# Three edits to a chunked recurrence kernel: which engine copies the transposed block inverses, which engine fills a block-diagonal tile, and when one product is placed on VectorE

## The chip, the cores and the metric

The kernel runs on one core of a Trainium2 chip. A core has TensorE (PE in the profile, with its weight loads as PEld), VectorE (DVE), ScalarE (ACT), GpSimd (POOL) and SyncE (SP), which here issues the DMAs. Each engine works through its own queue in order. The metric is device time in microseconds (us); lower is better. "q" behind an engine's name means its sequencer.

## The reference

Three layers follow one another. Nearly everything the change touches lies in the first, a recurrence over 768 tokens for 4 x 8 heads with a 40 x 40 state each:

```python
for t in range(S):
    y[:, :, t] = np.einsum('bhd,bhde->bhe', rt, state)
    Sa = np.einsum('bhde,bhe->bhd', state, at)
    state_decay = state * wt[:, :, None, :] - np.einsum('bhd,bhe->bhde', Sa, bt)
    state = state_decay + np.einsum('bhd,bhe->bhde', vt, kt)
...
h = np.maximum(x @ w_in, 0.0)              # second layer: 3-tap convolution over tokens, sigmoid gate
return (h * gate @ w_out).astype(np.float32)
...
gated = u * v_s                            # third layer: token mixing of a normalised half, then w_out
return (gated @ w_out).astype(np.float32)
```

All data are float32.

## The kernel before

The recurrence is computed in chunks. Tokens fall into 6 groups of 128 (two chunks of 64), and a group with one of the 4 batch entries is a unit, so there are 24 units of 8 heads. The main loop runs over the units; in pass `kk` it interleaves generators for different units in 19 parts, in the order of the string `CDCBDDCBDACAABBAADD`:

- A (unit `kk+9`): transposes `a` and P to make `bdA` and PT, and multiplies them (L174, masked into G at L175). PT comes from P by transposes on PE (L167), and P must by then be multiplied by the inverse decays `il` (function `l_pm`, L145, on VectorE).
- B (unit `kk+1`): builds `bdN`, a 128 x 128 tile per head that holds four 32 x 32 inverse blocks on its diagonal and two products beside them, and multiplies with it (L295, tile `pw`). The four diagonal quarters are copied from DT (L278); the block beside them is copied from `px` by ACT (L287). Before, quarters 1 and 3 are GpSimd's and quarters 0 and 2 VectorE's. There is one `bdN`.
- C (unit `kk`): the recurrence itself. For each of two chunks PE forms `pu` (L327), ACT copies it to ZU (L329), GpSimd copies that to UR (L331), PE forms the tile `pm` (L338, not the function `l_pm`), and VectorE adds and scales it (L339, L341). The next `pu` needs L341's output.
- D (units `kk-1` and `kk`): the output of the unit. Its masks are SS (L373).

Beside these, a generator `subst(n)` inverts the 32 x 32 triangular blocks of group n on VectorE, two operations per row (L206 multiplies, L208 adds), handed out at 1.25 operations per part. At its end a transposed copy LT of the inverses L is made (L211), stored to memory, and read back by `loadD` as DT. The group 0 copy of LT is VectorE's, those of groups 1 to 5 are ACT's. In group 0 (`SMALL`) a shorter form is used, and L278 is not executed.

The list SCHED says behind which part of a pass a prefetch step is put. `[5,"pm"]` puts `l_pm` behind part 5 of every odd pass up to pass 13 (of pass 1 four parts later), that is P for the pair of units whose A starts four parts on. VectorE, ACT and SP run in the order written here. From pass 14 on the weights of the second layer are split into high and low parts in the gaps (L551 to L604). The output of the recurrence goes through memory to the second and third layers, which run on PE at nearly full load.

Of the kernel before, what the change touches and what calls it, by code (L numbers as in the profile page):

```python
# [11 lines left out]
def attention(tc, keep, ident, vr,bk,w,a, x, spare=None):  # L12
    nc=tc.nc
    B,H,S,D=w.shape
    C=64; HB=32; NU=S//128; HC=C//2; H2=2*H; NP=B//2
    sy=nc.sync; V=nc.vector; T=nc.tensor; G_=nc.gpsimd; AC=nc.scalar
    with ExitStack() as ctx:
# [24 lines left out]
        for q in range(4):  # L42
            qs=slice(q*HB,(q+1)*HB)
# [43 lines left out]
        def later(m,f):  # L87
            due.append((now[0]+m,f)); 
        def tick():
            now[0]+=1  # L90
            for d in [d for d in due if d[0]<=now[0]]:
                due.remove(d); d[1]()
# [92 lines left out]
        def subst(n):  # L185
            if n not in Ls: Ls[n]=(sb.tile([128,HB*HB+HB],F32,name="L"),sb.tile([128,HB*HB//4],F32,name="tmp"),sb.tile([128,HB,HB],F32,name="LT"))
            flat,tmp,LT=Ls[n]
            L=flat[:,0:HB*HB].rearrange("p (t j) -> p t j",j=HB)
            BQ[0].dma_start(out=L,in_=tb_d[n])
            yield  # L190
            if n in SMALL:
                K=HB//2
                V.memset(L[:,K:,0:K],0.0)
                Q=flat.rearrange("p (s r) -> p s r",s=2)[:,:,0:K*HB].rearrange("p s (t j) -> p s t j",j=HB)[:,:,:,0:K]
                for j in range(1,K-1):
                    m=K-1-j
                    t=tmp[:,0:2*m*j].rearrange("p (s m k) -> p s m k",s=2,m=m)
                    V.tensor_tensor(t,Q[:,:,j+1:,j:j+1].to_broadcast([128,2,m,j]),Q[:,:,j:j+1,0:j].to_broadcast([128,2,m,j]),ALU.mult)
                    yield
                    V.tensor_tensor(Q[:,:,j+1:,0:j],Q[:,:,j+1:,0:j],t,ALU.add)  # L200
                    yield
            else:
                for j in range(1,HB-1):
                    m=HB-1-j
                    t=tmp[:,0:m*j].rearrange("p (m k) -> p m k",m=m)
                    V.tensor_tensor(t,L[:,j+1:HB,j:j+1].to_broadcast([128,m,j]),L[:,j:j+1,0:j].to_broadcast([128,m,j]),ALU.mult)  # L206
                    yield
                    V.tensor_tensor(L[:,j+1:HB,0:j],L[:,j+1:HB,0:j],t,ALU.add)  # L208
                    yield
            V.memset(flat[:,0:HB*HB:HB+1],1.0)  # L210
            (V.tensor_copy if n==0 else AC.copy)(LT,L.rearrange("p t j -> p j t"))  # L211
            def put():
                BQ[0].dma_start(out=dt_d[n],in_=LT)
                BQ[0].dma_start(out=dd_d[n],in_=L if n in SMALL else L[0:128:2])
                stored.update((n,j) for j in range(2))
            later(DDL,put)
            yield
        inv={}; stored=set()
        def loadD(p):

            if p>=NK//2: return
            n,j=p//2,p%2
            if (n,j) not in stored: return later(1,lambda: loadD(p))
            DT=sb.tile([128,H2,HB],F32,name="DT",bufs=1); D1=sb.tile([128,H2,HB],F32,name="D1",bufs=1)
            hs=slice(j*H2*4,(j+1)*H2*4)
            BQ[0].dma_start(out=DT,in_=dt_d[n][hs].rearrange("(b h q) t j -> (q t) (b h) j",b=2,q=4))
            if n in SMALL: BQ[0].dma_start(out=D1,in_=dd_d[n][hs].rearrange("(b h q) t j -> (q t) (b h) j",b=2,q=4))
            for c in range(0 if n in SMALL else 2):
                BQ[0].dma_start(out=D1[c*C:c*C+HB],in_=dd_d[n][j*H2*2:(j+1)*H2*2].rearrange("(b h q) t j -> q t (b h) j",b=2,q=2)[c])
            inv[n,j]=(DT,D1)  # L230
        def Bp(kk):

            i,n=units[kk]
            u=st[kk]; G=pair[n,i//2]['G']; h0=(i%2)*H
            DT,D1=inv[n,i//2]
            N=bdN[0]
            F=sb.tile([96,H,HB],F32,name="F",bufs=1)
            quarters=[slice(q*HB,(q+1)*HB) for q in range(4)]
            if n in SMALL:
                K=HB//2  # L240
                pe=ps.tile([128,H,K],F32,tag="ps",name="pe")
                for h in range(H):
                    for q,qs in enumerate(quarters):
                        T.matmul(pe[q*HB:q*HB+K,h],lhsT=G[qs,h0+h,q%2*HB:q%2*HB+K],rhs=DT[qs,h0+h,K:],start=True,stop=True)
                for q in range(4):
                    AC.copy(FI[q*HB:q*HB+K,:,K:],pe[q*HB:q*HB+K])
                yield
                pg=ps.tile([128,H,HB],F32,tag="ps",name="pg"); pd=ps.tile([96,H,HB],F32,tag="ps",name="pd")
                for h in range(H):
                    for qs in quarters: T.matmul(pg[qs,h],lhsT=D1[qs,h0+h],rhs=FI[qs,h],start=True,stop=True)  # L250
                for q in (1,3):
                    qs=quarters[q]
                    AC.copy(N[qs,:,q*HB:(q+1)*HB],pg[qs])
                for h in range(H):
                    for qs in quarters[::2]: T.matmul(pd[qs,h],lhsT=FI[qs,h],rhs=D1[qs,h0+h],start=True,stop=True)
                X0=sb.tile([96,H,HB],F32,name="X0",bufs=1)
                for q in (0,2):
                    qs=quarters[q]
                    V.tensor_copy(N[qs,:,q*HB:(q+1)*HB],pg[qs])
                    AC.copy(X0[qs],pd[qs])  # L260
                if i%2==1: later(DTLS,lambda: loadD(kk//2+1))
                yield
                right=lambda h,c: N[c*C+HB:c*C+C,h,c*C+HB:c*C+C]
                left=lambda h,lo: X0[lo,h]
            else:
                right=lambda h,c: DT[c*C+HB:c*C+C,h0+h]
                left=lambda h,lo: D1[lo,h0+h]
            pf=ps.tile([128,H,HB],F32,tag="ps",name="pf")
            for h in range(H):
                for c in range(2):  # L270
                    lo=slice(c*C,c*C+HB); hi=slice(c*C+HB,c*C+C)
                    T.matmul(pf[lo,h],lhsT=G[hi,h0+h,0:HB],rhs=right(h,c),start=True,stop=True)
            for c in range(2):
                lo=slice(c*C,c*C+HB)
                AC.copy(F[lo],pf[lo])
            for q in range(0 if n in SMALL else 4):
                qs=quarters[q]
                (G_.tensor_copy if q%2 else V.tensor_copy)(N[qs,:,q*HB:(q+1)*HB],DT[qs,h0:h0+H])  # L278
            yield
            px=ps.tile([128,H,HB],F32,tag="ps",name="px")  # L280
            for h in range(H):
                for c in range(2):
                    lo=slice(c*C,c*C+HB)
                    T.matmul(px[lo,h],lhsT=left(h,lo),rhs=F[lo,h],start=True,stop=True)
            for c in range(2):
                lo=slice(c*C,c*C+HB)
                AC.copy(N[lo,:,c*C+HB:c*C+C],px[lo])  # L287
            if i%2==1 and n not in SMALL: later(DTL,lambda: loadD(kk//2+1))
            yield
            WT=u['WT']=[]  # L290
            for g in range(2):
                W=sb.tile([104,4,128],F32,name="WT",bufs=4); WT.append(W)
                p=ps.tile([128,4,128],F32,tag="ps",name="pw")
                for j in range(4):
                    T.matmul(p[:104,j],lhsT=G[:,h0+g*4+j,C:],rhs=N[:,g*4+j],start=True,stop=True)  # L295
                AC.mul(W,p[:104],-1.0)
                yield
# [94 lines left out]
        def pump(m):  # L392
            while m>0 and (bg or bg2):
                q=bg or bg2
                try: next(q[0])
                except StopIteration: q.pop(0); continue
                m-=1
# [10 lines left out]
        with tc.manual_schedule(engines={mybir.EngineType.SP,mybir.EngineType.DVE,mybir.EngineType.Activation}):  # L408
# [30 lines left out]
            l4=lam_prep(4); next(l4)  # L439
            mixed(2,l2,W[3]); l_dup(2); l_g(2); mixed(3,l2,W[4]); flush()  # L440
            s0=subst(0); next(s0)
            lms['lam',2](); lms['lam',3]()
            next(l4)
# [12 lines left out]
            flush()  # L456
            l_il(4)
            sub1=subst(1); next(sub1)
            l_P(4)
            b0=Bp(0)  # L460
            for _ in range(4): next(b0); steps(l4,W[9])
            loadV(0)
# [7 lines left out]
            with tc.manual_schedule():  # L470
# [9 lines left out]
                for kk in range(NK):  # L480
                    i,n=units[kk]
# [6 lines left out]
                    for g in ORDER if kk<TAIL else ORDER2:  # L488
# [8 lines left out]
                        tick(); acc+=RATE0 if kk<3 else RATE if kk<14 else RATE2; pump(int(acc)); acc-=int(acc)  # L497
                        for s,f in SCHED[(kk+LA+1)%2]+SCHEDC[kk%2]:
                            if s==z:
# [20 lines left out]
RATE=1.25  # L520
RATE2=1.25
RATE0=1.4
SCHED=[[[1, "il"], [11, "araw"], [12, "ln"], [14, "g"], [15, "dup"], [16, "P"], [17, "ar"]], [[5, "pm"]]]
SCHEDC=[[[6, "Z"]], [[10, "V"]]]
SUB=5
TBL=3
# [543 lines left out]
```

## Time and profile before

| | |
|---|---|
| three runs | 956.01 us median (954.18 to 960.27) |
| the profiled execution | 954.4 us, of which the span is 952.7 us |
| PE busy over the span | 90% |
| VectorE, ACT, GpSimd busy | 70%, 56%, 21% |
| the recurrence's main loop | from about 95 to 476 us of the span |
| second and third layers | from about 476 us to the end |

A row of a timeline gives the start and the time taken in us, the engine, the line, the operation, the tiles written and read, the shape, and how many instructions are merged; in brackets stands how long the engine was idle just before and which instruction ended that idle time.

### The profile page before, as it was taken

To read this page: it belongs to the slowest core of one execution; us is meant where nothing else is said; L and a number is where in the kernel's file an instruction comes from. 1 tells how busy PE (TensorE), PEld (TensorE's weight loads), DVE (VectorE), ACT (ScalarE), POOL (GpSimd) and SP (SyncE) were. 2 spreads that over 40 slices of the span, in tenths; PEclk is the share of its full clock that TensorE was granted. 3 is DMA by queue.
4 is the path that set the end of the run, shared out by engine and by line. 5 is a ranking of instruction groups with operands and counts; after the bars stand their busy time and mean duration, and the time that the engine had idled before them with its cause. 6 is when DMAs were issued, how large, how long until landed. Compare 5 with 4: busy or idle time off the path is not lost. (4 is left out here: it accounts for less than half of the span.)

```text
span 952.7 us, 23475 instructions
## 1 busy us (share of the span) xinstructions
PE 855.6 (90%) x9575; PEld 791.0 (83%) x9575; DVE 662.5 (70%) x1503; ACT 536.8 (56%) x1166; POOL 204.7 (21%) x268
## 2 busy tenths in 40 slices
PE   0888689999989999899777799999999899998997
PEld 0577588988989888799766699998999889998997
DVE  6877784794876959876659976378725877368841
ACT  0463577768777765778555653366515654266521
POOL 2110011121211111233300102144123441234221
PEclk9975799999999998899889999999999999999999
DMA  8989794646557444244131320111001100011001
GB/s 216 211 208 208 158 207 110 152 97 155 112 115 161 90 121 112 79 130 113 60 108 66 98 81 26 36 49 35 27 22 42 57 0 26 21 53 32 1 1 46
DMA packets 149189, 86.70 MB, mean 91 GB/s; under 512 B 124176, under 2 KB 138256, under 8 KB 147152
## 3 DMA queue, kind: packets, MB, share of 16 engines
q1 hardware_dynamic: 148800, 84.78, 36.1%
q8 instruction: 77, 1.26, 0.6%
q14 instruction: 40, 0.33, 0.1%
q10 hardware_dynamic: 272, 0.33, 0.1%
HBM read 61.24 MB, written 23.86 MB: 89 GB/s over the span
## 5 line engine op out<-in xcount | busy, mean ns | idle before, releaser
L693 PE MATMUL psp<-spt,vv 128*128 128x384 f32 x576 | 105.6, 338 | 0.5 <-DVE vv L821 0.3
L693 PE MATMUL ph<-XT,G 128*128 128x386 f32 x512 | 102.6, 346 | 0.7 <-DVE XT L726 0.7
L693 PEld LDWEIGHTS psp<-spt,vv 128*128 128x128 f32 x576 | 100.2, 188 | 2.2 <-ACT vv L818 1.0
L693 PEld LDWEIGHTS ph<-XT,G 128*128 128x128 f32 x512 | 93.8, 194 | 1.1 <-DVE XT L726 1.0
L769 PE MATMUL acc<-gh,G 128*128 128x384 f32 x320 | 71.3, 349 | 16.0 <-ACT gh L753 9.3
L755 POOL TENSOR_TENSOR gl<-c,gh 128x384 fp32r<-128x384 f32 x48 | 66.2, 1379 | 89.8 <-ACT gh L753 78.2
L769 PEld LDWEIGHTS acc<-gh,G 128*128 128x128 f32 x320 | 56.5, 192 | 24.5 <-ACT gh L753 13.4
L331 POOL COPY ZU<-ZU 64x320 f32<-64x320 f32 x48 | 24.9, 519 | 222.8 <-ACT ZU L329 216.7
L838 DVE TENSOR_TENSOR psp<-psp,bb 128x384 f32<-128x384 f32 x32 | 18.1, 566 | 70.6 <-PE psp L693 70.5
L753 ACT CAST gh<-c 128x384 fp32r<-128x384 f32 x64 | 33.0, 515 | 52.2 <-DVE c L751 50.8
L751 DVE TENSOR_TENSOR c<-h,c 128x384 f32<-128x384 f32 x64 | 39.3, 613 | 33.2 <-ACT c L748 33.0
L208 DVE TENSOR_TENSOR L<-L,tmp 128x30 f32<-128x30 f32 (+9 forms) x150 | 57.6, 384 | 4.0
L174 PE MATMUL p<-PT,bdA 80*128 80x128 f32 x384 | 55.1, 304 | 3.4 <-ACT PT L168 3.3
L372 PE MATMUL pS<-bdR,ZV 80*128 80x128 f32 x384 | 55.3, 288 | 2.4 <-ACT ZV L366 2.4
L206 DVE TENSOR_TENSOR tmp<-L 128x30 f32<-128x30 f32 (+9 forms) x150 | 52.5, 350 | 7.0 <-DMA L<-tb 3.0
L174 PEld LDWEIGHTS p<-PT,bdA 80*128 80x128 f32 x384 | 51.7, 216 | 6.4 <-ACT PT L168 6.3
L295 PE MATMUL pw<-bdN,G 128*104 128x128 f32 x384 | 54.6, 303 | 1.2 <-issue 1.1
L842 ACT CAST zh<-u 128x384 fp32r<-128x384 f32 x28 | 14.4, 515 | 73.1 <-DVE u L839 73.1
L295 PEld LDWEIGHTS pw<-bdN,G 128*104 128x104 f32 x384 | 51.2, 196 | 2.1 <-issue 1.3
L175 DVE TENSOR_TENSOR G<-p,mT 128x512 f32<-128x512 f32 x48 | 32.8, 688 | 28.1 <-PE p L174 27.7
L372 PEld LDWEIGHTS pS<-bdR,ZV 80*128 80x128 f32 x384 | 47.7, 195 | 3.9 <-ACT ZV L366 2.8
L843 POOL TENSOR_TENSOR zl<-u,zh 128x384 fp32r<-128x384 f32 x28 | 28.6, 1022 | 101.0 <-ACT zh L842 89.8
(185 smaller groups left out, 2104.1 us busy)
## 6 DMA issues: line engine op xcount, KB each, us to landing
P<-in_bk_dram SPq DMA_DIRECT2D x12, 640.0 KB, 5.5
ZU<-in_vr_dram SPq DMA_DIRECT2D x12, 640.0 KB, 7.2
lq<-in_w_dram SPq DMA_DIRECT2D x12, 320.0 KB, 6.5
araw<-in_a_dram SPq DMA_DIRECT2D x12, 320.0 KB, 6.8
lam<-lq SPq DMA_DIRECT2D x12, 320.0 KB, 4.4
lnA<-lam SPq DMA_DIRECT2D x12, 320.0 KB, 7.4
ilam<-lq SPq DMA_DIRECT2D x12, 320.0 KB, 5.6
il<-ilam SPq DMA_DIRECT2D x24, 160.0 KB, 4.3
```

The lines of the kernel that those rows point to most:

```text
L174: T.matmul(p3[:,j],lhsT=bdA[:,g*4+j].rearrange("p c t -> p (c t)"),rhs=PTs[g][:,j],start=True,stop=True)
L175: V.tensor_tensor(G[:,hs,0:2*C],p3,mT.rearrange("p a t -> p (a t)").unsqueeze(1).to_broadcast([128,4,2*C]),ALU.mult)
L206: V.tensor_tensor(t,L[:,j+1:HB,j:j+1].to_broadcast([128,m,j]),L[:,j:j+1,0:j].to_broadcast([128,m,j]),ALU.mult)
L208: V.tensor_tensor(L[:,j+1:HB,0:j],L[:,j+1:HB,0:j],t,ALU.add)
L295: T.matmul(p[:104,j],lhsT=G[:,h0+g*4+j,C:],rhs=N[:,g*4+j],start=True,stop=True)
L372: T.matmul(p[:,j].rearrange("p c t -> p (c t)"),lhsT=ZV[:,j,0:2*C],rhs=bdR[:,j].rearrange("p c t -> p (c t)"),start=True,stop=True)
L693: L.tc.nc.tensor.matmul(out,lhsT=l,rhs=r,start=start and i==0,stop=stop and i==len(prs)-1)
L751: V.tensor_tensor(c,h[:,1:TH+1],c,ALU.mult)
L753: AC.copy(gh,c)
L755: def low(v): v.tensor_tensor(gl,c,gh.bitcast(F32),ALU.subtract)
L769: nc.tensor.matmul(acc[m],lhsT=l,rhs=r,start=f==0 and z<5 and z in (0,1,3),stop=f==NF-1 and z>=5)
L843: nc.gpsimd.tensor_tensor(gl,u,gh.bitcast(F32),ALU.subtract)
```

## The change

Three edits. LT is copied by VectorE in every group, where ACT made it for groups 1 to 5. All four quarters of `bdN` are copied by GpSimd, where two of them were VectorE's. And `l_pm` stands behind part 3 of the odd passes, where it stood behind part 5.

```diff
@@ subst
             V.memset(flat[:,0:HB*HB:HB+1],1.0)
-            (V.tensor_copy if n==0 else AC.copy)(LT,L.rearrange("p t j -> p j t"))
+            V.tensor_copy(LT,L.rearrange("p t j -> p j t"))
@@ Bp
             for q in range(0 if n in SMALL else 4):
                 qs=quarters[q]
-                (G_.tensor_copy if q%2 else V.tensor_copy)(N[qs,:,q*HB:(q+1)*HB],DT[qs,h0:h0+H])
+                G_.tensor_copy(N[qs,:,q*HB:(q+1)*HB],DT[qs,h0:h0+H])
@@ constants
-SCHED=[[...], [[5, "pm"]]]
+SCHED=[[...], [[3, "pm"]]]
```

On ACT one row goes at the end of each inversion; here in group 2, where the D part's ZV and the C part's ZU stand around it.

```order
@@ -151,5 +150,4 @@
 L362 ACTIVATE bdR<-pz,mB 80x4x64 x2
 L366 COPY ZV<-pv 80x4x104
-L211 COPY LT<-L 128x1024
 L329 COPY ZU<-pu 64x4x40 x2
 L287 COPY bdN<-px 32x8x32 x2
```

The ZU copy now stands right behind the ZV copy. VectorE takes LT behind the last step of the inversion and ahead of the second SS:

```order
@@ -264,4 +260,5 @@
 L373 TENSOR_TENSOR SS<-pS,mS 128x512
 L210 MEMSET L 128x32
+L211 COPY LT<-L 128x1024
 L373 TENSOR_TENSOR SS<-pS,mS 128x512
 L339 TENSOR_TENSOR pm<-pm,VM 40x320
```

The two instructions behind it, SS and the addition to `pm`, now stand behind LT. On VectorE in pass 5 (and 9 and 13) two `bdN` copies go and P's product moves up:

```order
@@ -224,10 +222,9 @@
 L206 TENSOR_TENSOR tmp<-L 128x238
 L208 TENSOR_TENSOR L<-L,tmp 128x14x17
-L278 COPY bdN<-DT 32x8x32 x2
 L206 TENSOR_TENSOR tmp<-L 128x234
+L145 TENSOR_TENSOR P<-P,il 128x1280
 L208 TENSOR_TENSOR L<-L,tmp 128x13x18
 L373 TENSOR_TENSOR SS<-pS,mS 128x512
 L206 TENSOR_TENSOR tmp<-L 128x228
-L145 TENSOR_TENSOR P<-P,il 128x1280
 L208 TENSOR_TENSOR L<-L,tmp 128x12x19
```

P's product stands ahead of SS and three steps of the inversion that it followed. PE's order is the same in both kernels, and so is SP's. On GpSimd each of the 20 bursts of copies doubles, always in the place of the first two; here one in the weight stretch (L604 is the low part of a weight):

```order
 L605 MEMSET G 64x512
 L331 COPY ZU<-ZU 64x8x40
-L278 COPY bdN<-DT 32x8x32 x2
+L278 COPY bdN<-DT 32x8x32 x4
 L331 COPY ZU<-ZU 64x8x40
 L604 TENSOR_TENSOR G<-mo,G 128x320 x2
```

Two more copies now stand ahead of the UR copy (L331) of the unit's second chunk.

## Rows read from the trace of the kernel before

**Rows 1.** The page: span, busy time of each engine over it.

```profile
span 952.7 us, 23475 instructions
PE 855.6 (90%) x9575; PEld 791.0 (83%) x9575; DVE 662.5 (70%) x1503; ACT 536.8 (56%) x1166; POOL 204.7 (21%) x268
```

**Rows 2.** Timeline at the LT copy of group 2: ACT, then PE.

```profile
216.66 1.98 ACT L211 COPY LT<-L 128x1024 f32<-128x1024 f32 x1 [0.84 <-DVE L L210]
218.54 0.60 ACT L329 COPY ZU<-pu 64x160 f32<-64x160 f32 x2
218.87 1.04 PE L338 MATMUL pm<-ZU,P 128*40 128x40 f32 x16 [1.00 <-ACT ZU L329]
```

**Rows 3.** Timeline of PE behind the LT copies of groups 1, 3 and 4.

```profile
154.41 1.08 PE L284 MATMUL px<-F,X 32*32 32x32 f32 x32 [0.85 <-ACT F L275]
...
280.96 1.04 PE L338 MATMUL pm<-ZU,P 128*40 128x40 f32 x16 [0.77 <-ACT ZU L329]
...
343.60 1.22 PE L338 MATMUL pm<-ZU,P 128*40 128x40 f32 x16 [0.98 <-ACT ZU L329]
```

**Rows 4.** Groups of instructions and, for bdN, by line (ns min/median/max): copies that move.

```profile
L211 ACT COPY LT<-L 128x1024 f32<-128x1024 f32 x5 | 9.9, 1978 | 8.1 <-DVE L L210 8.1
L211 DVE COPY LT<-L 128x1024 f32<-128x1024 f32 x1 | 1.0, 1044 | 0.0
L278 DVE COPY bdN<-DT 32x256 f32<-32x256 f32 x40 | 11.4, 284 | 0.5
L278 POOL COPY bdN<-DT x40: 394/401/767, 166.1 to 447.3; 32x256 f32<-32x256 f32 x40
```

**Rows 5.** Timeline at P's product in passes 5 and 13 (last).

```profile
201.83 1.49 DVE L145 TENSOR_TENSOR P<-P,il 128x1280 f32<-128x1280 f32 x1
203.46 1.04 PE L167 MATMUL p<-ident,P 128*80 128x128 f32 x8 [1.12 <-DVE P L145]
...
328.20 1.04 PE L167 MATMUL p<-ident,P 128*80 128x128 f32 x8 [1.11 <-DVE P L145]
```

**Rows 6.** Timeline at P's product in pass 1: the copy that completes il, and PE.

```profile
131.36 1.25 ACT L138 COPY il<-il 64x1280 f32<-64x1280 f32 x1
135.61 1.48 PE L167 MATMUL p<-ident,P 128*80 128x128 f32 x8 [1.93 <-DVE P L145]
```

**Rows 7.** Stretch 355 to 399 (times: span, PE, PEld, DVE, ACT, POOL; clock) and timeline at its ends.

```profile
355.00:399.00 44.00, 39.99 (x768) 36.98 (x762) 41.14 (x97) 29.23 (x72) 9.64 (x16) 0.92 0.41 104
354.93 0.51 DVE L339 TENSOR_TENSOR pm<-pm,VM 40x320 f32<-40x320 f32 x1 [1.62 <-PE pm L338]
400.02 1.08 PE L327 MATMUL pu<-VM,WT 104*64 104x40 f32 x16 [3.63 <-DVE VM L341]
```

**Rows 8.** Timeline: GpSimd and VectorE at the same time, in two places.

```profile
252.30 1.78 POOL L121 TENSOR_TENSOR G<-araw,lnA 128x640 f32<-128x640 f32 x1 [4.68 <-DVE L L208]
252.71 1.62 DVE L208 TENSOR_TENSOR L<-L,tmp 128x228 f32<-128x228 f32 x1
...
394.29 0.87 POOL L278 COPY bdN<-DT 32x256 f32<-32x256 f32 x2
394.93 0.41 DVE L206 TENSOR_TENSOR tmp<-L 128x168 f32<-128x168 f32 x1
395.38 0.33 DVE L208 TENSOR_TENSOR L<-L,tmp 128x168 f32<-128x168 f32 x1
```

**Rows 9.** Stretches behind two waits (all engines), then L295 alone at either clock (PE, PEld).

```profile
156.60:159.90 3.30, 3.30 (x18) 3.21 (x17) 0.66 (x2) 1.65 (x4) 0.00 (x0) 0.50 0.80 122
344.30:347.60 3.30, 3.30 (x23) 3.06 (x21) 1.64 (x6) 2.88 (x6) 0.14 (x1) 0.50 0.67 245
...
204.20:206.20 2.00, 1.86 (x16) 1.81 (x16) 1.00 0.73 124
374.36:378.10 3.74, 3.74 (x16) 3.41 (x16) 0.50 0.02 5
```

**Rows 10.** Timeline of PE at the second chunk of pass 5.

```profile
198.66 0.67 PE L327 MATMUL pu<-VM,WT 104*64 104x40 f32 x16 [0.20 <-DVE VM L341]
```

More of the change, by code (lines that the diff above doesn't have):

```diff
@@ L522 @@
 RATE0=1.4
-SCHED=[[[1, "il"], [11, "araw"], [12, "ln"], [14, "g"], [15, "dup"], [16, "P"], [17, "ar"]], [[5, "pm"]]]
+SCHED=[[[1, "il"], [11, "araw"], [12, "ln"], [14, "g"], [15, "dup"], [16, "P"], [17, "ar"]], [[3, "pm"]]]
 SCHEDC=[[[6, "Z"]], [[10, "V"]]]
```

## The prediction

> **What bounds the kernel now.** I read the busy times first: PE works for 90% of the span, VectorE for 70%, and the three engines between which the change shifts work are all below PE [rows 1]. So a copy that moves from one engine to another is worth nothing by its duration; it counts only where PE waits for the engine that loses or gets it. I therefore listed PE's idle times in the main loop and looked up in the timeline what ended each. Three kinds belong to this change.
>
> The first is the LT copy. In group 2 it holds ACT from 216.66 to 218.64, the ZU copy stands behind it, and PE waits 1.00 us for ZU [rows 2]. Groups 1, 3 and 4 show the same with 0.85, 0.77 and 0.98 us [rows 3]; in group 1 it is F that comes late. Group 5 shows no such wait.
>
> The second is P's product. In pass 5 it ends at 201.83+1.49=203.32 and PE, which has to transpose P, starts at 203.46 after 1.12 us of idling. Passes 5, 9 and 13 repeat this, 1.11 us in the last [rows 5]; pass 1 has it with 1.93 us [rows 6]. In passes 3, 7 and 11 PE does not wait there.
>
> The third is a VectorE that runs behind. From 354.93, when PE releases it, to 399 it is busy for 41.14 of 44 us, the rest being pauses between instructions, and at the end PE waits 3.63 us for L341 [rows 7]. In that stretch a microsecond taken from VectorE is one taken from the span.
>
> **The change part by part.**
>
> *LT to VectorE.* ACT loses 5 copies of 1.98 us and VectorE gets 5, of 1.04 us if they go as group 0's does [rows 4]. ACT was idle for 0.84 us before LT in group 2 [rows 2], so its ZU copy will run at once and be ready before PE asks: 1.00+0.85+0.77+0.98 = **3.60 us** gained. On VectorE the copy stands ahead of the second SS and of L339. L339 waits for PE's `pm` anyway, which starts at 218.87 [rows 2] and still at 217.87 without its wait, while LT, begun at about 216.6, is done by 217.7, and SS, 512 columns wide, takes some 0.6 us more (P's product takes 1.49 for 1280 [rows 5]). So I take its cost there as nothing; without that cover it would be 1.04 us for each of 5 copies, 5.2 us.
>
> *P's product two parts sooner.* In passes 5, 9 and 13 an SS, three steps of the inversion and two `bdN` copies no longer stand ahead of it. The steps alone are at least 0.33 us each [rows 8] and the copies 0.57, together 1.6, so it ends sooner by more than the three waits, of which the first has 1.12 us and the last 1.11: 3.3 us go. Behind it SS is late by 1.49 us, but the product that uses SS stands at the end of the pass. In pass 1 it can't start before ACT has completed `il` at 131.36+1.25=132.61, so it ends at about 132.65+1.48=134.1, PE starts about 0.14 us later at 134.3, having been free since 135.61-1.93=133.68: 0.6 us remain, 1.3 are gained. VectorE stands still there for some 0.3 us at most. Together **4.6 us**. No DMA is issued by this step; SP's next load into `il` waits for the product and so goes out earlier.
>
> *bdN to GpSimd.* VectorE loses 40 copies of 0.284 us, GpSimd gets 40 of 0.40 us in the median [rows 4]. GpSimd has time, 21% busy [rows 1]: a burst becomes 4 x 0.40 = 1.6 us, and `pw`, which needs all quarters, stands several microseconds later in the pass. Where VectorE runs behind, from 354.93 to 399, three pairs go: 3 x 0.57 = 1.7 us. Against this stands that both engines slow each other. Beside a copy of GpSimd the 168-column step took 0.41 us, without one 0.33 [rows 8]: 0.08 each, some 0.17 for a pair, in four bursts 0.7 us. The upper bound is the other pair of rows 8: L208 took 1.62 us beside the 1.78 us product of GpSimd, where by its 228 columns against 168 some 0.45 would do, so it stood still for about 1.2 us. I take the lower, since it is the same operation that is added, and net **1.0 us**.
>
> The Trainium skill (SBUF — State Buffer, Who interferes with whom) says that a DVE instruction with two SBUF inputs and a GpSimd instruction that reads SBUF exclude each other, and that the loser blocks for the whole of the other's instruction. By that rule a pair of added copies would hold VectorE for 0.80 us and not 0.17; the rows at 252 us agree with it, those at 394 us do not show it. It is a rival below.
>
> *The clock.* Behind two of the waits, at 154.41 and 343.60, stand stretches of 3.3 us with a granted clock of 0.50, the lower level (1.2 of 2.4 GHz) [rows 9]. The 16 products of L295 took 3.74 us at 0.50 and 1.86 at full clock [rows 9], so such a stretch costs 3.3/2 = 1.65 us. Waits of the same length at 218.87 and 280.96 have no such stretch behind them, so it is not sure that they come from these waits. Bounds: 0, and 3.3 us for both. In what precedes both I see nothing but the wait and take **3.3 us**.
>
> Sum: 3.6+4.6+1.0+3.3 = 12.5 us. The profiled execution took 954.4 us; 954.4-12.5 = 941.9. The median of the runs shown, 956.0, stands 1.6 above that execution, which gives **943.5 us**. After 400 us I expect no gain: PE is bound by its own work again, and the later layers only start earlier.
>
> **The rivals.**
>
> *The clock does not follow.* The waits go and the low stretches stay somewhere else: 954.4-9.2 = 945.2, with the 1.6 us 946.8. For it speaks that of four waits behind LT copies two have no low stretch behind them, as said.
>
> *VectorE takes the place of what goes.* In pass 5 PE already waits 0.20 us for L341 [rows 10], and nothing says VectorE can follow if PE runs 2 us sooner in each group. If copies on GpSimd hold it for their full 0.40 us, a burst costs VectorE 0.80-0.57 = 0.23 us instead of saving 0.40. In the stretch from 354.93 four bursts then lose 0.9 us instead of gaining 1.0, and in each of the three groups before, about 1.1 us of the waits for P come back as waits for L341: 12.5-1.9-3.3 = 7.3, 947.1, with the 1.6 us 948.7. With one low stretch left it would be 950.4. The rule of the skill above leads here. Against it stand the rows at 394 us.
>
> *Slower.* The same lock, but with the copies drawn out: GpSimd's slowest copy took 0.767 us [rows 4]. At x us held for each of two added copies a burst costs VectorE 2x-0.57. About 10 bursts lie where PE is near to waiting for it (four from 355, two in each of three groups). The gains that do not depend on this are 3.6+1.3+3.3 = 8.2 us, so from x = 0.70 on the change loses. At 0.767 in all of them it is 10 x 0.96 = 9.6, that is 954.4+1.4 = 955.8, with the 1.6 us 957.4. Against it: the median copy took 0.401.
>
> *No effect*, since other work of ACT would hold up ZU: excluded in group 2 by ACT's 0.84 us of idling.
>
> *More than forecast.* Behind the wait of 3.63 us the clock is low too: the 16 products of L327 at 400.02 took 1.08 us, those at 198.66 0.67 [rows 7, 10]. For how long no row here shows; were the wait short enough to spare 10 us of it, 5 more would go: 938.5.
>
> **How the numbers follow.** The forecast gets 0.50, more than it 0.07, the clock that does not follow 0.16, VectorE in its place 0.20, slower than before 0.07. The likeliest time is 943.5. The range from 937 to 952 takes in the first four and leaves out the slower case and some of the tail. A difference of 1% (9.6 us, here 946.4) is about what a measurement of this kernel tells from no change. Faster by more than that: the forecast nearly whole, the better case, and a little less than half of the clock's case, 0.60. Within 1%: the rest of the clock's case, VectorE in its place, and most of the slower case, 0.35. Slower by over 1%: 0.05.
>
> **What would show it.** Right: no wait for ZU or F behind the end of an inversion, no wait of `p` L167 for L145 but one of about 0.6 us in pass 1, L211 on VectorE at about 1.04 us, full clock around 157 and 344, and the wait at the fifth inversion's end nearer to 2.6 us than to 3.6. Wrong: new waits of `pu` for L341 in passes 4 to 13, L206 and L208 beside L278 at twice their times, `pw` waiting for GpSimd, or low stretches of as many microseconds as before.

## The result

| | kernel before | changed kernel |
|---|---|---|
| first series on one chip | 958.46 us median (954.18 to 964.22) | 950.88 us median (943.09 to 961.78) |
| ratio | | 0.9911, 95% interval 0.9887 to 0.9935 |
| the same again, later | 958.50 us | 951.09 us, ratio 0.9915 (0.9879 to 0.9951) |

The change makes the kernel faster by 0.9%, some 8 us. The ratio leaves out executions more than 1.5% above the fastest of their kernel, three of the twenty of the changed kernel here; with them the means are 951.3 and 958.3 us, a gain of 0.7%. I forecast 12.5 us, 1.3%. The profiled execution of the changed kernel was an unlucky one:

```profile
span 952.2 us, 23447 instructions
PE 863.1 (91%) x9575; PEld 798.7 (84%) x9575; DVE 657.1 (69%) x1468; ACT 525.4 (55%) x1161; POOL 221.5 (23%) x308
```

Its span is only 0.5 us below that of before [rows 1], while TensorE's busy time is 7.5 us longer for the same 9575 instructions: more of them ran at the low clock (mean granted clock 0.933, for 0.944). The executions of one kernel spread over up to 19 us, and a fit over 188 timed executions (one level for each kernel and series, one common slope) gives 4.9 us for 0.01 of mean granted clock. So these two profiles alone don't tell the result; a second one of the changed kernel (`after_again`) has a span of 944.2 us, and where the time is read by stage below, both stand.

The copies that moved, answering [rows 4], by line (duration in ns min/median/max, first and last start):

```profile
L211 DVE COPY LT<-L x6: 1039/1056/1165, 75.3 to 399.4; 128x1024 f32<-128x1024 f32 x6
L278 POOL COPY bdN<-DT x80: 390/398/856, 164.4 to 445.8; 32x256 f32<-32x256 f32 x80
```

Both are as long as the rows of before let expect. The ends of the first and fourth inversion, answering [rows 3] (timeline):

```profile
154.84 0.69 PE L284 MATMUL px<-F,X 32*32 32x32 f32 x32
...
341.50 0.61 ACT L329 COPY ZU<-pu 64x160 f32<-64x160 f32 x2
341.62 1.06 DVE L211 COPY LT<-L 128x1024 f32<-128x1024 f32 x1
343.60 0.81 PE L338 MATMUL pm<-ZU,P 128*40 128x40 f32 x16
```

No bracket stands behind L284 and L338 any more: ACT makes ZU while VectorE copies LT, and TensorE does not wait. Groups 2 and 3 read the same. P's product in passes 5 and 13, answering [rows 5], and what followed in pass 9:

```profile
200.72 1.07 PE L167 MATMUL p<-ident,P 128*80 128x128 f32 x8
...
273.54 0.66 PE L327 MATMUL pu<-VM,WT 104*64 104x40 f32 x16 [0.70 <-DVE VM L341]
...
329.19 1.07 PE L167 MATMUL p<-ident,P 128*80 128x128 f32 x8
```

The waits for P are gone, and a wait of `pu` for VectorE's L341 has come, 0.70 us. Pass 1, answering [rows 6]:

```profile
131.70 1.49 DVE L145 TENSOR_TENSOR P<-P,il 128x1280 f32<-128x1280 f32 x1
133.34 1.04 PE L167 MATMUL p<-ident,P 128*80 128x128 f32 x8 [0.94 <-DVE P L145]
135.96 1.35 ACT L315 COPY VM<-ZU 64x640 f32<-64x640 f32 x2 [2.38 <-DMA ZU<-in_vr_dram]
137.33 1.06 ACT L168 COPY PT<-p 80x512 f32<-80x512 f32 x2
137.96 2.94 PE L174 MATMUL p<-PT,bdA 80*128 80x128 f32 x16 [1.83 <-ACT PT L168]
```

TensorE waits twice: 0.94 us for P, then 1.83 us for PT, whose copy L168 stands on ACT behind L315, which waits for the load of ZU. Together 2.77 us, where it was 1.93 before. In the kernel before ACT had the same wait, and TensorE did not feel it (ACT, then PE):

```profile
137.77 1.35 ACT L315 COPY VM<-ZU 64x640 f32<-64x640 f32 x2 [3.24 <-DMA ZU<-in_vr_dram]
139.15 1.07 ACT L168 COPY PT<-p 80x512 f32<-80x512 f32 x2
...
136.88 3.19 PE L295 MATMUL pw<-bdN,G 128*104 128x128 f32 x16
139.90 1.95 PE L174 MATMUL p<-PT,bdA 80*128 80x128 f32 x16
```

Two things hid it there: TensorE's wait for P, and a stretch of 3.4 us at the low level from 136.1, in which L295 took 3.19 us. In the changed kernel L295 took 1.91 us (134.22); so at full clock the kernel before would, by an estimate from these two rows, have waited some 1.3 us for PT as well.

The stretch from 355 to 399 us, answering [rows 7] (columns: span, PE, PEld, DVE, ACT, POOL, granted clock, DMA share, GB/s):

```profile
355.00:399.00 44.00, 37.49 (x733) 34.45 (x731) 39.70 (x91) 27.48 (x67) 11.69 (x21) 0.95 0.42 103
```

The timeline of its start (VectorE) and of its end, with GpSimd's copies:

```profile
356.65 0.69 DVE L555 SCALAR_TENSOR_TENSOR mo<-mo,ct 128x512 f32<-128x512 f32 x1 [0.60 <-ACT mo L551]
360.80 0.20 DVE L206 TENSOR_TENSOR tmp<-L 128x30 f32<-128x30 f32 x1 [1.07 <-DMA L<-tb]
...
392.64 1.88 POOL L278 COPY bdN<-DT 32x256 f32<-32x256 f32 x4
393.39 0.41 DVE L206 TENSOR_TENSOR tmp<-L 128x168 f32<-128x168 f32 x1
398.63 1.08 PE L327 MATMUL pu<-VM,WT 104*64 104x40 f32 x16 [3.84 <-DVE VM L341]
```

VectorE has 1.4 us less to do in it (39.70 for 41.14), yet the wait at its end is 3.84 us, for 3.63. What VectorE saved it now waits itself: 0.60 us for ACT's `mo` and 1.07 us for the load of L, with which the next inversion begins. Before, VectorE had no wait above 0.2 us between the `pu` at 357.28 and the one at 400.02. Last the clock, answering [rows 9] (columns as for the stretch above):

```profile
156.60:159.90 3.30, 3.30 (x33) 3.30 (x31) 0.71 (x2) 2.77 (x6) 0.80 (x1) 1.00 0.60 112
344.30:347.60 3.30, 3.30 (x33) 3.26 (x31) 1.73 (x6) 2.92 (x7) 0.00 (x0) 1.00 0.49 166
302.80:316.40 13.60, 13.60 (x121) 12.45 (x118) 7.03 (x17) 6.01 (x15) 0.62 (x1) 0.50 0.35 80
138.90:149.10 10.20, 10.20 (x198) 9.40 (x201) 5.04 (x15) 3.66 (x11) 0.45 (x1) 0.50 0.39 75
```

The two stretches at 0.50 of which the forecast spoke run at full clock now. Two others have come: one behind pass 1's double wait, one at 302.8 us.

### The profile page after: what moved, and what is told of

The parts are those of the page before. It is cut to its first block, busy times and chain, and to the rows that moved or that the text cites. A ratio compares the mean times of both kernels' runs of the same rounds, so it can differ in the third digit from the quotient of the medians.

```text
span 952.2 us, 23447 instructions
## 1 busy us (share of the span) xinstructions
PE 863.1 (91%) x9575; PEld 798.7 (84%) x9575; DVE 657.1 (69%) x1468; ACT 525.4 (55%) x1161; POOL 221.5 (23%) x308
## 3 DMA queue, kind: packets, MB, share of 16 engines
q8 instruction: 77, 1.26, 0.6%
## 5 line engine op out<-in xcount | busy, mean ns | idle before, releaser
L331 POOL COPY ZU<-ZU 64x320 f32<-64x320 f32 x48 | 26.4, 550 | 195.9 <-ACT ZU L329 195.9
L372 PE MATMUL pS<-bdR,ZV 80*128 80x128 f32 x384 | 57.7, 297 | 2.5 <-ACT ZV L366 2.4
L329 ACT COPY ZU<-pu 64x160 f32<-64x160 f32 x96 | 27.5, 286 | 48.6 <-PE pu L327 45.8
L372 PEld LDWEIGHTS pS<-bdR,ZV 80*128 80x128 f32 x384 | 50.0, 203 | 4.0 <-ACT ZV L366 2.8
L295 PE MATMUL pw<-bdN,G 128*104 128x128 f32 x384 | 50.7, 289 | 1.2 <-issue 1.1
```

What stands on the lines that cost most here:

```text
L372: T.matmul(p[:,j].rearrange("p c t -> p (c t)"),lhsT=ZV[:,j,0:2*C],rhs=bdR[:,j].rearrange("p c t -> p (c t)"),start=True,stop=True)
```

## Experiments

### Each part alone, and two together

```diff
 lt_alone:  -(V.tensor_copy if n==0 else AC.copy)(LT,...)  +V.tensor_copy(LT,...)
 bdn_alone: -(G_.tensor_copy if q%2 else V.tensor_copy)(N[qs,...  +G_.tensor_copy(N[qs,...
 p_alone:   -SCHED=[[...], [[5, "pm"]]]  +SCHED=[[...], [[3, "pm"]]]
 lt_and_p:  the first and the third
 lt_and_bdn: the first and the second
```

> Of the three edits only the first: VectorE copies LT in every group. Theory of waits: PE's four waits behind LT (3.60 us) go, VectorE shows no new wait of PE, and 3.5 to 5 us are gained (ratio 0.995 to 0.9965), more if low-clock stretches follow the waits. Rival, VectorE takes its place: the 1.04 us copy comes back as waits of `pu` for L341 behind each inversion, and the ratio is 0.998 to 1.003.

> Only the second edit: GpSimd copies all four quarters of bdN. Theory of waits: no wait of PE goes or comes but the one at 400 us; VectorE saves 1.7 us of copies in the stretch from 355 us and loses about 0.5 us to copies beside its steps; 0 to 1 us gained (ratio 0.999 to 1.000). In the trace of the changed kernel the saving went into two new waits of VectorE (1.4 us), so 0 is likelier. Rival, the two engines block each other for whole copies: 2 to 5 us lost (1.002 to 1.005).

> Only the third edit: P's product behind part 3. Theory of waits: the three waits of 1.1 us in passes 5, 9 and 13 go, and in pass 1 the wait for P is exchanged for one on PT behind the ZU transfer; 2.5 to 3.5 us gained (ratio 0.9965 to 0.9975). With bdN's copies still on VectorE the product starts 0.57 us later than in the changed kernel and still ends before PE asks for it. Rival, the earlier product delays L341: waits of `pu` grow by up to 0.5 us in passes 5, 9 and 13, and under 2 us are gained.

> The first and the third edit without the second. Theory of waits: 6 to 8.5 us gained, as much as with all three (ratio 0.991 to 0.994), since GpSimd's copies count for nothing. Rival, bdN's copies on GpSimd are what makes room on VectorE: without them PE waits for L341 in passes 6, 10 and 14 by 0.5 to 1.2 us each, and 2 us of the gain are missing (0.994 to 0.996).

> Two parts of the change without the third: L's copies on VectorE, bdN's on GpSimd, P's product where it stood. It tells what P's product sooner is worth inside the whole, which stood at 0.9911 and 0.9915 of the kernel before. Theory (P's waits and VM's trade for each other, and pass 1 loses as much as passes 5, 9 and 13 gain): P's wait in those passes stands at about 0.47 us each, as with bdN's part alone, pu waits less than 0.2 us for VM there, pass 1 shows one wait for P near 1.9 to 2.5 us and none for PT; the ratio is 0.989 to 0.993, the same as the whole. Rival (P's part pays its 3.3 us and more): the ratio is 0.995 or above.

| kernel | median us | ratio to before, 95% interval | mean granted clock, that of before beside it |
|---|---|---|---|
| `lt_alone` | 952.32 | 0.9864 (0.9812 to 0.9917) | 0.942, 0.936 |
| `bdn_alone` | 958.83 | 0.9965 (0.9926 to 1.0004) | 0.938, 0.936 |
| `p_alone` | 962.91 | 1.0004 (0.9969 to 1.0039) | 0.935, 0.936 |
| `lt_and_p` | 952.58 | 0.9913 (0.9874 to 0.9953) | 0.940, 0.936 |
| `lt_and_bdn` | 945.08 | 0.9879 (0.9828 to 0.9930) | 0.945, 0.939 |
| all three, again | 951.09 | 0.9915 (0.9879 to 0.9951) | 0.940, 0.939 |

The ratios are not quotients of these medians; before's medians beside them were 961.60 us (first four rows), 957.01 and 958.50 us.

LT's part carries the gain: by these ratios it is worth 1.4% alone (1.0% by the medians), 0.9% beside P's part and 0.9% beside bdN's. P's part is worth nothing that the totals show, alone or added to LT's part or to LT's and bdN's together, where the ratio gets larger (0.9864 to 0.9913, 0.9879 to 0.9911). That it does harm is not shown, since the intervals overlap. bdN's part comes out at 0.35% alone, with an interval that just reaches no change, and adds nothing clear of the intervals to LT's (0.9864 to 0.9879) or to LT's and P's (0.9913 to 0.9911).

Of the expectations, that for `lt_and_p` met its range. `lt_alone` gained more than expected (0.995 to 0.9965, more with the clock): its four waits of 3.60 us and some 3.0 us by the clock (below) make 0.993, which lies outside its interval of six executions. Where the rest comes from is not shown. `p_alone` came out above its 0.9965 to 0.9975, on the side of its rival; the 0.999 to 1.000 for `bdn_alone` lie inside its interval.

Why P's part gives nothing is in the timeline of `p_alone`:

```profile
139.10 3.61 PE L174 MATMUL p<-PT,bdA 80*128 80x128 f32 x16 [2.37 <-ACT PT L168]
...
268.28 1.07 PE L167 MATMUL p<-ident,P 128*80 128x128 f32 x8
...
280.58 0.67 PE L327 MATMUL pu<-VM,WT 104*64 104x40 f32 x16 [0.98 <-DVE VM L341]
...
345.01 0.67 PE L327 MATMUL pu<-VM,WT 104*64 104x40 f32 x16 [0.74 <-DVE VM L341]
```

and the stretch behind its first row (columns as above):

```profile
139.40:152.90 13.50, 13.50 (x282) 12.61 (x282) 6.71 (x19) 5.26 (x16) 0.45 (x1) 0.50 0.40 70
```

P no longer makes TensorE wait in pass 9 (268.28), but L341 does behind it, and in pass 13 as well: VectorE's rows follow one another there without a pause, steps of the inversion ahead of L339 and L341. Pass 1 gets the wait for PT, and 13.5 us at the low level behind it. And in `lt_and_bdn`, where P's product stands at its old place:

```profile
203.86 1.04 PE L167 MATMUL p<-ident,P 128*80 128x128 f32 x8 [0.50 <-DVE P L145]
325.68 1.04 PE L167 MATMUL p<-ident,P 128*80 128x128 f32 x8 [0.50 <-DVE P L145]
```

The waits for P have shrunk to less than half of [rows 5] without P's product being moved: bdN's part alone takes two copies (0.57 us) from ahead of it. TensorE's idle time (gaps with neither matmul nor weight load, a few hundredths under the brackets) at these two places in passes 5, 9 and 13; the 0.2 us of [rows 10], which every kernel has, and standstills that no engine ends are left out:

| kernel | before P's transposes | before `pu`, for L341 | sum |
|---|---|---|---|
| before, `lt_alone` | 1.08, 1.08, 1.08 | none | 3.24 |
| `p_alone` | none | 0, 0.95, 0.71 | 1.66 |
| `lt_and_p` | none | 0, 0.95, 0.72 | 1.67 |
| `bdn_alone`, `lt_and_bdn` | 0.47, 0.47, 0.47 | 0, 0.19, 0 | 1.60 |
| all three, two executions | none | 0, 0.67, 0 and 0, 0.43, 0.43 | 0.67, 0.86 |
| all three with `v_later`'s edit (below) | none | 0.43, 0.69, 0.43 | 1.55 |

Where a kernel with P's part shows 0, TensorE had mostly just lost time otherwise (in pass 5 a standstill of 1.11 us in `p_alone`, 0.39 in `lt_and_p`, 0.97 and 0.46 in the whole; 13.6 us of low clock ahead of the whole's pass 13), so these sums are low. bdN's part by itself takes off 1.6 us, P's at most that, and both together 1.7 to 2.6, not 3.2. The two remove the same lateness of VectorE, and where only the order changes, the wait changes its place.

The time by stage, from the starts of TensorE's `pu`; in parentheses microseconds at the low level in it. The stages go, in before's times, from 128.69 (pass 1) to 164.24 (pass 3), to 303.13 (pass 12), to 357.28 (pass 15), to 410.90 (pass 19).

| kernel | passes 1-2 | 3-11 | 12-15 | 15-19 |
|---|---|---|---|---|
| before | 35.55 (6.8) | 138.88 (0) | 54.15 (3.4) | 53.62 (17.1) |
| `p_alone` | 39.52 (17.1) | 140.91 (6.8) | 54.56 (6.8) | 53.92 (17.1) |
| `bdn_alone` | 33.55 (3.4) | 137.20 (0) | 54.85 (3.4) | 53.28 (17.1) |
| `lt_alone` | 32.81 (6.8) | 138.01 (3.4) | 52.65 (0) | 55.09 (17.1) |
| `lt_and_bdn` | 32.07 (6.8) | 135.41 (0) | 51.27 (0) | 54.91 (17.1) |
| all three | 34.62 (10.2) | 135.72 (0) | 57.11 (13.7) | 52.83 (10.2) |
| all three, again | 32.16 (6.8) | 135.52 (0) | 51.59 (0) | 53.40 (13.7) |

Passes 1-2 do not compare as they stand: `lt_alone`, `lt_and_bdn` and the second trace of all three start them 3.2, 4.4 and 2.2 us later than before did, with 14 to 17 us more at the low level ahead of them, and found P ready. Passes 3 to 11, where the last three rows have no low clock, are the cleanest place: without P's part 135.41 us, with it 135.72 and 135.52. Less the standstills there (0.29 us, 0.97 and 1.05) that is a gain of 0.4 to 0.7 us by P's part. The expectation for `lt_and_bdn` (the same as the whole, P's waits of 0.47) held there; the single wait for P in pass 1 that it named was missing, and its total, 0.9879, was below the range I had written (0.989 to 0.993).

### The wait for PT in pass 1

Theory: the order on ACT makes it. Rival: P is late anyway. `v_later` moves ACT's copies of ZU into VM four parts later, `v_12` two; `v_later_2` is `v_later` once more, and `after_again` the changed kernel.

```diff
-SCHEDC=[[[6, "Z"]], [[10, "V"]]]
+SCHEDC=[[[6, "Z"]], [[14, "V"]]]
```

> The changed kernel once more, unchanged, beside the three below on one chip and with a trace of its own. It tells what of the low-clock stretches belongs to the kernel and what to the single execution. Theory (the clock follows the waits): the waits stand where they stood (0.91 and 1.83 us in pass 1, 0.2 to 0.7 us of pu for VM, 3.8 us near 395 us), no low-clock stretch lies behind the places of the four old LT waits, one does behind pass 1's 1.83 us; ratio to before 0.988 to 0.994. Rival (the clock is luck of the single execution): stretches of 3 us or more also near 157 or 344 us, none behind pass 1, and a ratio anywhere from 0.99 to 1.00.

> The changed kernel with loadV, ScalarE's copies of ZU into VM, four places later in the pass. In pass 1 PT's copies stand behind such a copy, which waits for the load of ZU, and TensorE waits 1.83 us for PT, with 10.2 us of low clock behind it. Theory (that order makes the wait that took the place of P's): the 1.83 us wait falls to 0.5 us or less, the low stretch behind it to 3.4 us or none, and the time is 2 to 5 us under the changed kernel's in the same call, 0.995 to 0.998 of it. Rival (P itself comes late, PT's copies would wait anyway; or VM comes late for pu then): the wait for PT stays over 1.2 us, or pu gains waits for VM of 0.5 us and more in pass 1 and behind it; the time is within 1 us of the changed kernel's.

> The changed kernel with loadV two places later instead of four. Theory (ScalarE's order makes the wait for PT in pass 1): where TensorE comes to pass 1 at full clock, the wait for PT is 0.6 us or less in place of 1.83; ratio to before 0.986 to 0.991. Rival (the 2.9 us between v_later and the changed kernel were spread): 0.991 to 0.994, with or without the wait.

> The changed kernel with loadV four places later, once more, since six executions of it stood at 0.9896 with an interval from 0.9853 to 0.9939 beside the changed kernel's 0.9915. Theory (its wait for PT in pass 1 is gone for good): 0.987 to 0.9905, below the changed kernel. Rival (spread, or other stalls take the gain): 0.991 to 0.994.

The timeline of `v_later` in pass 1 and behind it:

```profile
134.56 1.04 PE L167 MATMUL p<-ident,P 128*80 128x128 f32 x8 [0.94 <-DVE P L145]
137.19 1.95 PE L174 MATMUL p<-PT,bdA 80*128 80x128 f32 x16
138.01 1.35 ACT L315 COPY VM<-ZU 64x640 f32<-64x640 f32 x2
...
147.01 0.79 PE L255 MATMUL pd<-D,FI 32*32 32x32 f32 x32 [2.44 <-issue]
```

and the stretch behind it:

```profile
147.50:161.00 13.50, 13.50 (x154) 12.29 (x147) 4.25 (x10) 6.60 (x16) 0.48 (x1) 0.50 0.43 112
```

The wait for PT is gone, in `v_12` and `v_later_2` too: that order makes the wait is shown. A gain is not: each of the three traces has a standstill of 2.44, 1.40 and 1.98 us at L255 instead, ended by no other engine (the first trace of the changed kernel has none there, seven other traces 0.5 to 0.9 us), and 13.5 us of low clock behind it, so that passes 1 and 2 took 35.9 to 36.9 us, more than before. The total was 0.9896 (0.9853 to 0.9939), 0.9899 (0.9867 to 0.9932) and 0.9899 (0.9859 to 0.9939), 948.2 to 948.6 us. All three points lie below those of the changed kernel, but inside its interval.

`after_again` was to tell what belongs to the kernel. The stretches behind the old LT waits are at full clock again, but in this execution the low clock held from 56.4 to 121.3 us, TensorE came to pass 1 4 us later and at the low level there, and found P and PT ready: no wait of either kind, and 6.8 us of low clock. So pass 1's double wait is there in some executions only, which the rival had in part.

### Filling the waits of pass 1

```diff
+                        if kk==1 and g=='A':
+                            nA+=1
+                            if nA in FILL: warm(ident,FILL[nA])
+FILL={2:6,4:12}
```

> The changed kernel with eighteen matmuls more, whose results nothing reads: six ahead of the wait for P in pass 1 and twelve ahead of the wait for PT. At 0.13 us each at full clock (the eight transposes of L167 take 1.04) they fill 0.8 of the 0.91 us and 1.6 of the 1.83 us, so the operands come when they came and only TensorE's idle time goes. Theory (the low clock behind pass 1 follows TensorE's standing still): where TensorE comes to these places at full clock, the low stretch of 10.2 us behind them falls to 3.4 us or none and the next passes come 1.5 to 4 us sooner; ratio to before 0.986 to 0.990. Rival (the low clock there does not hang on these waits): 10 us or more stay behind them, and the time is that of the changed kernel or, where TensorE comes there late and has nothing to wait for, up to 4 us longer: 0.991 to 0.996.

```profile
136.04 2.93 PE L407 MATMUL warm<-ident 128*128 128x128 f32 x12
138.76 1.47 PE L167 MATMUL p<-ident,P 128*80 128x128 f32 x8
141.82 2.84 PE L407 MATMUL warm<-ident 128*128 128x128 f32 x24
```

Inconclusive. The six and twelve matmuls run as 12 and 24 and took 2.93 us at the low clock and 2.84 at full, where I had reckoned 0.8 and 1.6 us from the transposes. TensorE also came there at the low level already, behind a standstill of 1.52 us at 129 us. The wait and the clock were not parted. The time, 0.9881 (0.9837 to 0.9925), lies in the theory's range, but says only that 5.8 us of idle matmuls in pass 1 cost nothing that can be measured.

### What sets the wait at the fifth inversion's end

```diff
-EX=[3, 7, 7, 9, 11, 15, 19, 22, 26, 28]
+EX=[3, 3, 3, 5, 9, 14, 19, 22, 26, 28]
```

> The changed kernel with another row of numbers for how many steps of the weights' conversion are done by each pass: 3, 3, 3, 5, 9, 14 where 3, 7, 7, 9, 11, 15 stood, so that six of them leave the stretch from 355 to 400 us, in which VectorE makes the carry that TensorE waits 3.6 to 3.8 us for at the end of the fifth inversion. Theory (VectorE's backlog sets that wait): it falls to 2.5 us or less and VectorE's stretch from carry to carry from 44.4 to 42 us or less; 1 to 3 us are gained over the changed kernel, up to 2 more where the clock follows. Rival (the chain of the carry, with its waits for ScalarE and DMA, sets it): the wait stays within 3.3 to 4.2 us and the time within 1 us; or the conversions, done later, are waited for behind 400 us and the time is 1 to 3 us longer.

> The changed kernel with both, loadV later and the six steps later. If both theories hold it gains the sum, 3 to 8 us on the changed kernel, 0.980 to 0.988 of the kernel before; if only the one in pass 1 holds, 2 to 5 us; if neither, it is within 1 us of the changed kernel.

`ex_later` came to 0.9917 (0.9883 to 0.9950), the changed kernel's time. `v_ex`, the same together with `v_later`'s edit, came to 0.9994 (0.9968 to 1.0021). In `v_ex` the stage from pass 15 to 19 fell to 50.95 us, 1.9 us under the best of the table above, in `ex_later` only to 52.33. From the `pu` of pass 15 to that at the fifth inversion's end VectorE was busy for 34.88 and 35.11 us in them and for 38.95 in the changed kernel; the stretch took 40.96, 42.43 and 43.18 us, of which 6.8, 6.8 and 3.7 us at the low level. So 4 us taken from VectorE shortened it by 0.8 to 2.2: VectorE's load sets it in part only. The rest VectorE spends waiting, for TensorE's `pS` and for the load of L, as the rival had it in part (timelines of `v_ex`, then `ex_later`):

```profile
359.49 0.69 DVE L373 TENSOR_TENSOR SS<-pS,mS 128x512 f32<-128x512 f32 x1 [1.65 <-PE pS L372]
363.00 0.21 DVE L206 TENSOR_TENSOR tmp<-L 128x30 f32<-128x30 f32 x1 [1.73 <-DMA L<-tb]
...
366.29 0.20 DVE L206 TENSOR_TENSOR tmp<-L 128x30 f32<-128x30 f32 x1 [2.98 <-DMA L<-tb]
```

The inversion so ends later against TensorE: its copy LT starts 3.5 us behind that `pu` in both, 0.8 in the changed kernel. Behind it TensorE waits anew (timeline of `v_ex`):

```profile
411.71 0.69 PE L272 MATMUL pf<-DT,G 32*32 32x32 f32 x32 [1.42 <-DMA DT<-dt]
428.69 1.04 PE L338 MATMUL pm<-ZU,P 128*40 128x40 f32 x16 [1.52 <-ACT ZU L329]
```

with some 10 us at the low clock behind each; the next stage, to 460.54 in before, took 61.91 us for 49.64. So 1.9 us are gained and 12.3 lost, in an execution 6.6 us above its median. The trace of `ex_later` has the first of these waits with 1.25 us, the second with 0.46, and 56.39 us for that stage. Why its time was still the changed kernel's stays open: the trace is of an execution 8.5 us above its median.

No kernel of these is shown to beat the changed one. The lowest ratios are those of `lt_alone`, 0.9864, and `lt_and_bdn`, 0.9879, both without the third edit.

## Why the prediction was right or wrong

The sign came as forecast and the time within the range, 950.9 of 937 to 952, with two thirds of the gain: by its ratio 947.5 on the 956.0 from which I started, for 943.5. I had given 0.60 to more than 1%; it is 0.9%, with an interval that ends at 1.13%. That the time fell within the range is in part luck: LT's part alone brings the whole gain, and P's 4.6 us, over a third of the sum, are not there. By its steps:

**LT to VectorE, 3.6 us: right.** All four waits went, the copy took 1.06 us (taken: 1.04), no wait came in behind it. The stages show it: with LT's part alone passes 12-15 fall by 1.5 us, and 3-11 by 0.9 in spite of 3.4 us of low clock; of the 2.7 us in passes 1-2 some 1.9 are the wait for P, which TensorE, coming later, did not meet. Some of it is given back: the stage from pass 15 to 19 is 1.5 us longer, as it is in `lt_and_bdn` (1.3). VectorE waits there for the load of L, 1.06 and 1.04 us, which it did not before; the rest is open.

**P's product, 4.6 us: wrong; this is the step that failed.** Two things were overlooked.
- In passes 5, 9 and 13 I counted the whole 3.3 us because the product ends soon enough. It does. But VectorE works there without a pause, and whatever TensorE stops waiting for at P, it meets again at L341, up to 0.98 us in one pass. I saw that as the rival "VectorE takes the place" and priced it through contention between the engines; it needs none. Half of the wait was also bdN's to take: beside bdN's part, P's edit is worth 0.1 to 0.9 us there (1.60 less 1.55 to 0.67), where I had put 3.3.
- In pass 1 I forecast a wait of 0.6 us; it was 0.94. I looked only at what P waits for, not at what TensorE wants next. The load of ZU, ACT's L315 behind it and PT's copy behind that would have been late in the kernel before as well; the wait for P and the low clock behind it hid it. Taking 1 us off one wait uncovered 1.83 of another in the profiled execution. It is 2.37 in `p_alone` and 1.75 in `lt_and_p`, with 13.5 us of low clock behind it in the first and none in the second, and there is no such wait in `after_again`.

**bdN to GpSimd, 1.0 us: the size is not excluded, the place was wrong.** In the stretch from 355 to 399 us VectorE lost 1.4 us of work, but the wait at the end did not shrink (3.63 to 3.84; 1.99 in `after_again`, with 3.0 us of other waits earlier in the stage, for 1.4 before). My premise that a microsecond taken from VectorE there is one taken from the span was wrong: VectorE then waits itself, 0.60 us for `mo` and 1.07 for the load of L; the stage from pass 15 to 19 is 0.2 to 0.8 us shorter than before's in the whole, 0.3 with bdN's part alone. Its gain is in passes 3 to 11, 1.7 us alone, through P's waits. The contention was taken about rightly: the 168-column step took 0.41 us beside four copies of 1.88 us, 0.33 without, and no step lost more than 0.29 us. The rule of the Trainium skill (SBUF — State Buffer, Who interferes with whom), by which a VectorE instruction would be held for the whole of such a copy, is not what this trace shows: no step beside them was held for 0.40 us.

**The clock, 3.3 us: the places were right, the size was that of one execution.** Of the twelve waits behind LT in the traces of before, `p_alone` and `bdn_alone`, four are followed by a low stretch within 3 us, two of them in before: on the average 1.3 in a trace, which at 1.65 us each is 2.2 us. With LT on VectorE these waits are gone, and a low stretch stands at their places only where TensorE stood still for another reason. At 4.9 us for 0.01 the mean granted clocks give 3.0 us for LT alone (0.942 for 0.936), 3.1 for LT and bdN and 0.5 for all three, with standard errors of 1.4, 1.3 and 0.9, so that they hardly differ. If the clock was lost elsewhere with all three, pass 1's wait for PT, which only P's part makes, would fit, but that it causes this is not shown: `fill`, which was to show it, told nothing. And much of the low clock lies ahead of passes 1-2, where its length differs from execution to execution, 58.0 and 64.9 us in the two of the changed kernel.

**The rivals.** "Slower" and "No effect" are out. On 956.0 the result, 947.5, lies between "The clock does not follow" (946.8) and "VectorE takes the place" (948.7). The second had the right mechanism without the lock on which I let it hang; of the first it is not shown how far it holds, since the clock followed at its two places and may have been lost in pass 1. Of the low stretch that "More than forecast" hoped to shorten, 10.2 us in before, 6.8 us stayed in both traces.

**The tell-tales.** No wait for ZU or F, L211 at 1.06 us, full clock at 157 and 344: as said. The wait at the fifth end and pass 1: not as said. Of the signs for "wrong", `pu` waiting for L341 came, and low stretches as long as before in one of two traces: 34.1 and 20.5 us in the four stages of the table, 27.3 before.

## What to carry to other kernels

When a wait is taken away, ask for what TensorE would have waited next, on every engine and load whose lateness that wait was hiding; here, in the profiled execution, a load behind a copy cost more than what was taken off the wait. Where one engine feeds TensorE without a pause, a product moved ahead in its order only moves the wait; take work off that engine instead (and look what it will itself have to wait for then), and don't add up two edits that remove the same lateness. And time each part alone, and the whole without each part: an edit that removes its wait in the trace can be worth nothing.

## What the runs showed of the hardware

TensorE stands still in the middle of a run of equal matmuls, with no engine or DMA in the trace that it waits for. The timeline of the changed kernel, behind which the stretch at 302.80 shown with the result begins:

```profile
300.58 0.59 PE L272 MATMUL pf<-DT,G 32*32 32x32 f32 x25
302.66 0.38 PE L272 MATMUL pf<-DT,G 32*32 32x32 f32 x7 [1.49 <-issue]
```

The timeline of `bdn_alone` at the same place:

```profile
301.59 0.62 PE L272 MATMUL pf<-DT,G 32*32 32x32 f32 x26
304.21 0.31 PE L272 MATMUL pf<-DT,G 32*32 32x32 f32 x6 [2.00 <-issue]
```

and the stretch behind it:

```profile
304.50:318.00 13.50, 13.50 (x229) 12.72 (x229) 10.96 (x23) 10.67 (x22) 2.76 (x3) 1.00 0.38 82
```

In ten of fourteen traces such a standstill falls on these matmuls near 302 us, 0.4 to 2.0 us long. The page of the changed kernel has a DMA queue of instructions (packets, MB, share of 16 engines):

```profile
q8 instruction: 77, 1.26, 0.6%
```

One of its packets, of 1.3 us, ends where the standstill at 302 us begins, and one of 1.4 us where that of 210 us does; most of the 77 have no standstill behind them. The Trainium skill (Runtime: NRT & Kernel Launch, Instruction fetch mechanics) says that a sequencer fetches its instructions itself in blocks of 16 KiB while it executes the block before, and that the cost is mostly hidden. The size agrees (1.26 MB / 77 = 16 KB). That the standstills are a fetch that was not hidden is a guess which no run here tested.

The clock does not follow the length of a standstill: behind 1.49 us it was at the lower of its two levels (1.2 of 2.4 GHz) for 13.6 us, behind 2.00 us at the same place it stayed at full. Two executions of the same kernel differed by 8 us in span (952.2 and 944.2), 5.5 of it in passes 12 to 15, where this happened in one and not in the other.
